# V by whole token tiles, one norm's transposes on VectorE through DRAM, and two chunks' head outputs split elsewhere, in a two-layer attention and Mish kernel

## The chip, the cores and the metric

The kernel runs on one core of one Trainium2 chip. The metric is the time of one execution on the device in microseconds (us), given as the median of several runs. PE is TensorE (the matrix engine), DVE is VectorE, ACT is ScalarE, POOL is GpSimd, and SP is SyncE, which here only issues DMAs.

## The reference

Everything is fp32. The sequence has 2048 tokens of width 512; there are 32 heads of width 16, and the hidden width of the dense part is 1792. The same weights serve both layers.

```python
def layernorm(x):  # no weights, eps 1e-5
    return (x - mean(x)) / sqrt(var(x) + eps)

def attention(x, wqkv, wo):
    q, k, v = (x @ wqkv) as 32 heads of 16
    p = softmax(q @ k.T * 16 ** -0.5)
    return heads(p @ v) @ wo

def dense(x, w1, b1, w2):
    h = x @ w1 + b1
    return (h * tanh(softplus(h))) @ w2      # Mish

x = A_x
for layer in range(2):
    x = x + attention(layernorm(x), A_wqkv, A_wo)
    x = x + dense(layernorm(x), B_w1, B_b1, B_w2)
```

## The kernel before, in words

**Tiles and precision.** Tokens are worked on in four chunks of 512 (NCH = 4), each of four tiles of 128. An fp32 product is made of three matmuls: each operand is split into a high part, rounded to the faster fp32r type, and a low part, the rest (`mm3`, L199 to L201: high by high, low by high or high by low). A split is a copy on ACT (or POOL) that makes the high part and a subtraction on DVE that makes the low part (`split_psum`, L193 and L194).

**Norm.** Two forms exist. `norm_parts` takes statistics on DVE (L228, L229), the inverse root on POOL (L210, L211), the scaled rows on DVE (L218), transposes them on PE (L248), and splits the result out of PSUM. `norm_units` does the same with DVE transposes (L298), stores on SP's queue to a DRAM buffer (L302), one load back (L311), and splits in SBUF (L314 on ACT, L315 on DVE). It is a generator whose steps are hung between other work. Its scaled and transposed tiles take places under the tag `raw` (three places), which every second projected tile `pt` of the next stage uses too.

**QKV.** `qkv` projects Q and K by pairs (m, c) in a written order: m is a group of 128 output features (0 to 3 are Q, 4 to 7 are K), c a token chunk. Each pair is one PSUM bank `qk` of twelve matmuls, split into `pt` (ACT, DVE) and stored to the DRAM buffer `scr` from ACT's queue. A dictionary `within` says ahead of which pair and step other functions run. In the second layer the first place where the last chunk (c = 3) is needed is the twelfth pair, (0, 3); its norm, called `late`, runs inside this order. V of chunks 0 to 2 follows (`va`); V of chunk 3 (`vp`, `v_parts` with `paired`) is drawn into the first steps of the attention. The function `behind` pins an instruction's place in the order; PE's instructions are chained in the written order in the second layer.

**Attention.** 8 groups of 4 heads, 4 query chunks, 16 key tiles of 128 make 512 steps (STEPS). Softmax subtracts a row maximum, which is worked out ahead of its use: a half step of maximum (`max_mm`, item M) makes two matmuls into one two-bank tile `pm` (tag `mx`, two buffers) and one DVE reduce (L404); every 32 of them end in `max_fold`. Score matmuls come in pairs (`sp`, L452, item P, tag `s2`) and singles (`ss`, L462, item S, tag `s1`), whose exp on ACT goes to `p` (L453, L463); `pv` matmuls (L478) sum p times V in one bank, which `drain` copies to `ot` (L499 to L503) and stores to `oscr`. Tiles `p` live in the shared pool of 8 KB places (`b8`), from which many other tiles come too, so that a `p` can take the place of any older tile. The items run in a fixed cycle of three steps. The pool of the score banks is opened with

```python
with tc.tile_pool(name="sa", bufs=1, space=PSUM, reuse_waits="tile") as self.pool:
```

At the attention's start, the first 2 PRE items M are not maxima but two `k` steps of V each (L520 to L522).

**Head outputs.** `HeadsOut` of a chunk loads the unnormalised sums (`num`) and the denominators (`den`) from `oscr`, inverts the denominators on DVE (`invert`, L664), sends them through DRAM (`rscr`) and spreads them over the features of each head (`spread`, `rec`), multiplies (L676), and splits into `oh` (POOL, L679) and `ol` (DVE, L680). Chunks 0 to 2 do this at hooks counted from the last step:

```python
for c, (t0, t1, t2, t3) in enumerate(((-42, -38, -36, -20), (-29, -21, -20, -13), (-13, -9, -8, None))):
```

They are the steps of load, inversion, spread and `parts` (product and split); chunk 2's `parts` come behind the loop. `project(c)` then multiplies by wo (`wo_parts`, 48 matmuls a chunk) and adds the residual (L718). The dense part follows, with hidden tiles `h` (L733) and output tiles `mo` (L759).

Of the kernel before, what the change touches and what calls it, by code (L numbers as in the profile page):

```python
# [18 lines left out]
P = 128  # L19
S, D, H, DH, F = 2048, 512, 32, 16, 1792  # L20
NCH = 4
# [57 lines left out]
def kernel(ctx: ExitStack, tc: tile.TileContext, x, wqkv, wo, w1, b1, w2, out):  # L79
# [244 lines left out]
    class Attention:  # L324
# [166 lines left out]
        def drain(self):  # L491
            b, self.full = self.full, None
            if b is None:
                return
            g, qb = divmod(b, NCH)
            ot = t512("f", f"ot{self.l}{b}")
            acc = self.accs.pop(b)
            if b == NG * NCH - 1:
                behind(nc.vector.tensor_copy(ot, acc))  # L499
            elif self.l and qb < NCH - 1:  # L500
                nc.scalar.activation(mixed(ot), grouped(acc), AF.Copy)  # L501
            else:
                nc.scalar.activation(ot, acc, AF.Copy)  # L503
            self.stored = nc.sync.dma_start(self.oscr[qb][g // 2, g % 2], ot)

        def run(self, hooks, pre):
# [3 lines left out]
            with tc.tile_pool(name="sa", bufs=1, space=PSUM, reuse_waits="tile") as self.pool:  # L510
                half, done = 2 * (AHEAD + PRE), -4
                for s in range(STEPS + 4):
                    if s % GSTEPS == GSTEPS - NKT and s // GSTEPS + 1 < NG:
                        self.prep_v(s // GSTEPS + 1)
                    for item in CYCLE[s % 3]:
# [3 lines left out]
                        elif item == "S":  # L519
                            self.single()  # L520
                        elif item == "M" and left:
                            left -= 1  # L522
                            next(pre)
                            next(pre)
                            if not left:
                                next(pre, None)
                                self.prep_v(0, [NCH - 1])
                        elif item == "M":
                            self.max_mm(half // 2, half % 2)
                            half += 1  # L530
                        else:
                            done += 1
                            self.pv(units(done))
# [113 lines left out]
    class HeadsOut:  # L647
# [14 lines left out]

        def invert(self):
            behind(nc.vector.reciprocal(self.den, self.den))  # L664
            for q in range(NCH):
                behind(nc.gpsimd.dma_start(self.rscr[:, ts(q, P)], self.den[ts(q, H)]))
# [6 lines left out]

        def parts(self):
            nm = f"{self.l}{self.c}"
            behind(nc.vector.tensor_tensor(self.num, self.num, self.rec, op=ALU.mult))  # L676
            oh = b8([P, KT, CW], F32R, "oh" + nm)
            ol = b8([P, KT, CW], F32R, "ol" + nm)
            nc.gpsimd.tensor_copy(oh, self.num)  # L679
            behind(nc.vector.tensor_tensor(ol, self.num, oh.bitcast(F32), op=ALU.subtract))  # L680
            self.out = oh, ol

        def pieces(self):
# [150 lines left out]
    for l in range(2):  # L834
# [10 lines left out]
        else:  # L845
            order = [(0, 0), (0, 1), (4, 0), (4, 1), (1, 0), (0, 2), (4, 2), (1, 1), (1, 2), (5, 0), (5, 1), (0, 3), (4, 3)]
            att = attention(1)
            att.chained = True
            late = norm_parts(x2s[NCH - 1], f"q1{NCH - 1}", tt, NCH - 1, "mx", True, pe=att.pe)
            for at in ((4, 0), (4, 0), (9, 0), (9, 2)):  # L850
                within.setdefault(at, []).append(lambda: next(late))
        order += [(m, c) for m in (1, 5, 2, 6, 3, 7) for c in range(NCH) if (m, c) not in order]
# [32 lines left out]
        outs = [HeadsOut(l, c, att.oscr) for c in range(NCH)]  # L885
        for c, (t0, t1, t2, t3) in enumerate(((-42, -38, -36, -20), (-29, -21, -20, -13), (-13, -9, -8, None))):
            o = outs[c]
            at(STEPS + t0, o.load)
            at(STEPS + t1, o.invert)
            at(STEPS + t2, o.spread)  # L890
# [8 lines left out]
        outs[3].load()  # L899
        outs[2].parts()  # L900
        load_res(1)
# [4 lines left out]
        load_res(3)  # L906
        for _ in project(0):
            pass
        first = norm_parts(x2s[0], f"m{l}0", tts, 0, "s", pin=behind, pe=att.pe, halves=True)
# [72 lines left out]
```

## Time and profile before

| | |
|---|---|
| Median of 3 runs | 3493.39 us (3493.02 to 3493.46) |
| Profiled execution | 3493.51 us |
| Its span | 3491.7 us |
| Granted TensorE clock, mean | 1.000 of full speed |
| PE busy | 3478.3 us, 100% of the span |
| DVE busy | 3001.3 us, 86% |
| ACT busy | 2572.9 us, 74% |
| POOL busy | 240.2 us, 7% |
| DMA | 274.99 MB, mean 79 GB/s |
| Largest groups | DVE max reduce L404 2384.2 us; ACT exp L453 1396.5 us; PE pv L478 1165.7 us; PE maximum L400 1099.0 us |

A group line of the profile reads: source line, engine, operation, output<-inputs with their shapes, how often, then its busy time and the mean of one, then the idle time of its engine ahead of it and what ended most of it. In a timeline row the first two numbers are the start and the duration in us; the bracket at the end is the idle time of the engine ahead of the row and what released it. Matmuls are pipelined, so the duration of one is longer than the distance to the next, and distances between starts are used for PE. Names without numbers stand for all tiles of that name.

### The profile page before, as it was taken

The numbers are of one execution on the slowest core, as the hardware profiler recorded it, in microseconds if no ns is written. First come the engines' busy times: TensorE is split into PE (matmuls) and PEld (weight loads), VectorE is DVE, ScalarE is ACT, GpSimd is POOL, SyncE is SP. The second block draws the span as 40 slices with busy tenths as digits, with TensorE's granted clock in tenths as the row PEclk, the third lists the DMA queues.
The fourth block names the chain that finished last, engine by engine and source line by source line (L and its number), as shares of the span: only waits on it lengthen the run. The fifth ranks groups of instructions, "written<-read, shape, count | busy, mean of one in ns | idle before, by whom it ended". The sixth has DMA issues, their size and how long they took to land.

```text
span 3491.7 us, 68687 instructions
## 1 busy us (share of the span) xinstructions
PE 3478.3 (100%) x28572; PEld 1921.3 (55%) x28572; DVE 3001.3 (86%) x3166; ACT 2572.9 (74%) x3513; POOL 240.2 (7%) x392
## 2 busy tenths in 40 slices
PE   9999999999999999999999999999999999999999
PEld 7644444444444444888876444444444444448887
DVE  6689999999999996667756999999999999956675
ACT  3288888888888889356622888888888888884565
POOL 3100010001001002100010000000000000021000
PEclk9999999999999999999999999999999999999999
DMA  7741323222131314722374203111120312156210
GB/s 248 234 91 44 64 60 75 50 53 72 51 63 56 65 36 91 231 69 73 109 224 151 45 21 58 34 35 34 32 48 21 54 27 45 21 113 213 76 37 25
DMA packets 185268, 274.99 MB, mean 79 GB/s; under 512 B 72117, under 2 KB 114037, under 8 KB 171133
## 3 DMA queue, kind: packets, MB, share of 16 engines
q1 hardware_dynamic: 158036, 193.95, 22.8%
q10 hardware_dynamic: 19176, 43.06, 3.6%
q0 software_dynamic: 7744, 33.60, 3.4%
q8 instruction: 224, 3.67, 0.5%
q14 instruction: 88, 0.71, 0.1%
HBM read 158.87 MB, written 110.62 MB: 77 GB/s over the span
## 4 chain that ended last, share of the span: by engine, by line
PE 96%; DMA 1%; DVE 1%; ACT 1%; issue 0%; POOL 0%; SPq 0%; DVEq 0%; ACTq 0%; POOLq 0%
PE pv L478 30%; PE pm L400 18%; PE ss L462 13%; PE sp L452 9%; PE h L733 8%; PE mo L759 8%; PE qk L199 2%; PE qk L200 1%; PE qk L201 1%; PE va L199 1%; PE wo L199 1%; PE wo L201 1%; PE wo L200 1%; PE va L201 1%; PE va L200 1%; DMA vscr<-v 0%
## 5 line engine op out<-in xcount | busy, mean ns | idle before, releaser
L404 DVE TENSOR_REDUCE mxv<-pm 128x2 f32<-128x1024 f32 x2048 | 2384.2, 1218 | 148.4 <-PE pm L400 96.0
L453 ACT ACTIVATE p<-sp 128x1024 f32<-128x1024 f32 x1366 | 1396.5, 1022 | 10.6 <-DMA vscr<-v 2.7
L478 PE MATMUL pv<-p,va 128*32 128x256 f32 (+2 forms) x16032 | 1165.7, 392 | 0.6 <-ACT ot L501 0.4
L400 PE MATMUL pm<-ks,qs 48*128 48x512 f32 x4096 | 1099.0, 446 | 1.6 <-DVE mxv L404 1.3
L463 ACT ACTIVATE p<-ss 128x512 f32<-128x512 f32 x1364 | 815.3, 598 | 338.6 <-PE ss L462 258.1
L452 PE MATMUL sp<-qs,ks 50*128 50x512 f32 x2732 | 738.1, 445 | 0.5 <-ACT p L453 0.5
L478 PEld LDWEIGHTS pv<-p,va 128*32 128x32 f32 x16032 | 368.3, 108 | 504.9 <-issue 424.4
L400 PEld LDWEIGHTS pm<-ks,qs 48*128 48x128 f32 x4096 | 451.8, 184 | 347.2 <-issue 234.1
L462 PE MATMUL ss<-qs,ks 50*128 50x512 f32 x1364 | 610.6, 448 | 1.5 <-ACT p L463 1.5
L462 PEld LDWEIGHTS ss<-qs,ks 50*128 50x128 f32 x1364 | 252.1, 185 | 329.4 <-ACT p L463 238.1
L452 PEld LDWEIGHTS sp<-qs,ks 50*128 50x128 f32 x2732 | 267.0, 183 | 184.4 <-ACT p L453 108.5
L421 POOL CAST hi<-nt 128x32 fp32r<-128x32 f32 x64 | 13.3, 208 | 2263.1 <-DVE nt L417 2263.1
L736 ACT ACTIVATE hb<-h,b1t 128x512 f32<-128x512 f32 x112 | 77.2, 689 | 101.6 <-PE h L733 100.7
L740 ACT ACTIVATE hr<-he 128x512 f32<-128x512 f32 x112 | 70.8, 632 | 104.6 <-DVE he L739 104.6
L193 ACT ACTIVATE pt<-qk 128x512 fp32r<-128x512 f32 x64 | 38.2, 597 | 143.4 <-PE qk L201 102.0
L743 DVE TENSOR_TENSOR hb<-hb,hr 128x512 f32<-128x512 f32 x112 | 77.4, 691 | 45.0 <-ACT hr L741 42.9
L737 DVE TENSOR_SCALAR he<-hb 128x512 f32<-128x512 f32 x112 | 47.5, 424 | 79.8 <-ACT hb L736 73.8
L747 DVE TENSOR_TENSOR al<-hb,ah 128x512 fp32r<-128x512 f32 x112 | 77.4, 691 | 28.8 <-ACT ah L746 23.1
L746 ACT ACTIVATE ah<-hb 128x512 fp32r<-128x512 f32 x112 | 70.2, 627 | 29.9 <-DVE hb L743 29.9
L739 DVE SCALAR_TENSOR_TENSOR he<-he 128x512 f32<-128x512 f32 x112 | 76.7, 685 | 17.2 <-ACT he L738 17.2
L194 DVE TENSOR_TENSOR pt<-qk,pt 128x512 fp32r<-128x512 f32 x64 | 43.8, 685 | 53.7 <-ACT pt L193 51.6
L741 ACT ACTIVATE hr<-hr,lnhalf 128x512 f32<-128x512 f32 x112 | 81.1, 724 | 3.6
(224 smaller groups left out, 3000.5 us busy)
## 6 DMA issues: line engine op xcount, KB each, us to landing
scr<-pt ACTq DMA_DIRECT2D x64, 512.0 KB
qs<-scr SPq DMA_DIRECT2D x174, 128.0 KB
ks<-scr SPq DMA_DIRECT2D x174, 128.0 KB
vscr<-v SPq DMA_DIRECT2D x32, 512.0 KB
va<-vscr SPq DMA_DIRECT2D x64, 256.0 KB
oscr<-ot SPq DMA_DIRECT2D x64, 256.0 KB
ww<-sw POOLq DMA_DIRECT2D x14, 1024.0 KB, 4.3
num<-oscr SPq DMA_DIRECT2D x64, 128.0 KB
```

Of the source, the lines that this page charges most:

```text
L199: pe(nc.tensor.matmul(acc, ah, bh, start=first and i == 0, stop=False))
L200: pe(nc.tensor.matmul(acc, ah, bl, start=False, stop=False))
L201: pe(nc.tensor.matmul(acc, al, bh, start=False, stop=last and i == n - 1))
L400: nc.tensor.matmul(pm[:, e], qs[u][rows, q0 : q0 + P], ks[u][rows, ts(n, 512)], start=True, stop=True)
L404: nc.vector.tensor_reduce(self.mxs[b][:, 2 * u : 2 * u + 2, qt, n], pm, axis=AX.X, op=ALU.max)
L452: self.pe(nc.tensor.matmul(sp[:, e], k, q, start=True, stop=True))
L453: nc.scalar.activation(self.pts[-1][:, 0:n], sp[:, 0:n], AF.Exp, scale=SCALE)
L462: self.pe(nc.tensor.matmul(sp, k, q, start=True, stop=True))
L463: nc.scalar.activation(self.pts[i // 3][:, 2], sp, AF.Exp, scale=SCALE)
L478: nc.tensor.matmul(self.accs[b][ts(h, VW), cols], self.va[b // NCH][:, kt, h, :], self.pts[j][:, e, cols], start=kt == 0 and q0 == 0, stop ...
L733: pe(nc.tensor.matmul(acc, w[:, part, k, ts(f % 2, P)], t[:, k, :], start=i == 0, stop=i == 3 * KT - 1))
L759: nc.tensor.matmul(obs[c][t // 2][:, t % 2], act[:, ts(t, P)], w[:, part, f % 2], start=f == part == 0 and act is ah, stop=f == FT - 1 and ...
```

## The change

1. V of the last chunk, both layers: in place of two `k` steps at each of the items M ahead of the maxima, all four `k` steps of one token tile (twelve matmuls) run at every second such item, and none at the others.
2. The second layer's last norm (`late`): `norm_units` takes the place of `norm_parts`; its steps run ahead of pairs 0 to 9 of the order.
3. Head outputs. Chunk 0's inversion is done in four quarters at four successive steps, and its spread moves from step −36 to −34. Chunk 1's product and split leave the loop (step −13) and come behind it, ahead of chunk 2's product; its cast moves from POOL to ACT. Chunk 2's split moves to the middle of the first projection.
4. In the second layer, `ot` is evicted through the `mixed` and `grouped` views for the fourth query chunk as well.

```diff
--- before.py
+++ after.py
@@ -495,12 +495,11 @@
             g, qb = divmod(b, NCH)
             ot = t512("f", f"ot{self.l}{b}")
             acc = self.accs.pop(b)
+            to, acc = (mixed(ot), grouped(acc)) if self.l else (ot, acc)
             if b == NG * NCH - 1:
-                behind(nc.vector.tensor_copy(ot, acc))
-            elif self.l and qb < NCH - 1:
-                nc.scalar.activation(mixed(ot), grouped(acc), AF.Copy)
+                behind(nc.vector.tensor_copy(to, acc))
             else:
-                nc.scalar.activation(ot, acc, AF.Copy)
+                nc.scalar.activation(to, acc, AF.Copy)
             self.stored = nc.sync.dma_start(self.oscr[qb][g // 2, g % 2], ot)
 
         def run(self, hooks, pre):
@@ -520,8 +519,8 @@
                             self.single()
                         elif item == "M" and left:
                             left -= 1
-                            next(pre)
-                            next(pre)
+                            for _ in range(KT * (left % 2)):
+                                next(pre)
                             if not left:
                                 next(pre, None)
                                 self.prep_v(0, [NCH - 1])
@@ -660,9 +659,10 @@
             for h in range(P // DH):
                 nc.sync.dma_start(self.num[ts(h, DH)], rows[:, h, 0:DH].rearrange("k d n -> d k n"))
 
-        def invert(self):
-            behind(nc.vector.reciprocal(self.den, self.den))
-            for q in range(NCH):
+        def invert(self, i=0, n=1):
+            part = ts(i, P // n)
+            behind(nc.vector.reciprocal(self.den[:, part], self.den[:, part]))
+            for q in range(NCH if i == n - 1 else 0):
                 behind(nc.gpsimd.dma_start(self.rscr[:, ts(q, P)], self.den[ts(q, H)]))
 
         def spread(self):
@@ -671,14 +671,23 @@
             for h in range(P // DH):
                 behind(nc.gpsimd.dma_start(self.rec[ts(h, DH)], rows[:, h][None].to_broadcast([DH, KT, CW])))
 
-        def parts(self):
+        def product(self):
+            return nc.vector.tensor_tensor(self.num, self.num, self.rec, op=ALU.mult)
+
+        def split(self, cast):
             nm = f"{self.l}{self.c}"
-            behind(nc.vector.tensor_tensor(self.num, self.num, self.rec, op=ALU.mult))
             oh = b8([P, KT, CW], F32R, "oh" + nm)
             ol = b8([P, KT, CW], F32R, "ol" + nm)
-            nc.gpsimd.tensor_copy(oh, self.num)
+            if cast is nc.scalar:
+                cast.activation(oh, self.num, AF.Copy)
+            else:
+                cast.tensor_copy(oh, self.num)
             behind(nc.vector.tensor_tensor(ol, self.num, oh.bitcast(F32), op=ALU.subtract))
             self.out = oh, ol
+
+        def parts(self):
+            behind(self.product())
+            self.split(nc.gpsimd)
 
         def pieces(self):
             nm = f"{self.l}{self.c}"
@@ -846,9 +855,9 @@
             order = [(0, 0), (0, 1), (4, 0), (4, 1), (1, 0), (0, 2), (4, 2), (1, 1), (1, 2), (5, 0), (5, 1), (0, 3), (4, 3)]
             att = attention(1)
             att.chained = True
-            late = norm_parts(x2s[NCH - 1], f"q1{NCH - 1}", tt, NCH - 1, "mx", True, pe=att.pe)
-            for at in ((4, 0), (4, 0), (9, 0), (9, 2)):
-                within.setdefault(at, []).append(lambda: next(late))
+            late = norm_units(x2s[NCH - 1], f"q1{NCH - 1}", tt, NCH - 1)
+            for n in (0, 0, 0, 0, 1, 2, 3, 4, 6, 8, 9):
+                within.setdefault((n, 0), []).append(lambda: next(late))
         order += [(m, c) for m in (1, 5, 2, 6, 3, 7) for c in range(NCH) if (m, c) not in order]
         qkv(l, att, wts, tt, order, within, due)
         if l == 0:
@@ -883,10 +892,12 @@
         for i in range(2):
             at(STEPS - 9 + 2 * i, lambda i=i: wot.append(ready(f"wo{i}", l)))
         outs = [HeadsOut(l, c, att.oscr) for c in range(NCH)]
-        for c, (t0, t1, t2, t3) in enumerate(((-42, -38, -36, -20), (-29, -21, -20, -13), (-13, -9, -8, None))):
+        for c, (t0, t1, t2, t3) in enumerate(((-42, -38, -34, -20), (-29, -21, -20, None), (-13, -9, -8, None))):
             o = outs[c]
             at(STEPS + t0, o.load)
-            at(STEPS + t1, o.invert)
+            n = NCH if c == 0 else 1
+            for i in range(n):
+                at(STEPS + t1 + i, lambda o=o, i=i, n=n: o.invert(i, n))
             at(STEPS + t2, o.spread)
             if t3 is not None:
                 at(STEPS + t3, o.parts)
@@ -897,15 +908,18 @@
         att.run(hooks, v_parts(l, NCH - 1, wts, tt, att, True))
         load_res(0)
         outs[3].load()
-        outs[2].parts()
+        behind(outs[1].product())
+        behind(outs[2].product())
+        outs[1].split(nc.scalar)
         load_res(1)
         load_w1(0)
         load_res(2)
         load_w2(0)
         load_w1(1)
         load_res(3)
-        for _ in project(0):
-            pass
+        for i, _ in enumerate(project(0)):
+            if i == NCH * KT // 2:
+                outs[2].split(nc.gpsimd)
         first = norm_parts(x2s[0], f"m{l}0", tts, 0, "s", pin=behind, pe=att.pe, halves=True)
         for i, _ in enumerate(project(1)):
             for n in range({0: 1, 8: 1, 11: 2, 14: 2}.get(i, 0)):
```

## The prediction

> **What bounds the kernel now.** I read the page first: busy shares, then the chain that ended last.
>
> ```profile
> span 3491.7 us, 68687 instructions
> PE 3478.3 (100%) x28572; PEld 1921.3 (55%) x28572; DVE 3001.3 (86%) x3166; ACT 2572.9 (74%) x3513; POOL 240.2 (7%) x392
> PE 96%; DMA 1%; DVE 1%; ACT 1%; issue 0%; POOL 0%; SPq 0%; DVEq 0%; ACTq 0%; POOLq 0%
> ```
>
> TensorE carries 96% of the chain and is idle for 13 us in all (3491.7 − 3478.3). So only two things can shorten the program: fewer or cheaper steps on PE, or the removal of a wait on PE. The change adds no matmul to PE and takes away only the 16 transposes of one norm. Everything else in it is worth what it does to PE's waits, and I looked at each place in the timeline by engine. The profiled execution took 3493.51 us, 1.81 around its span, and the median of the runs is 3493.39, so a difference worked out on the span is taken off the median as it stands. About 0.2% (7.0 us) is what a measurement of this kernel can tell from no change.
>
> **V by whole token tiles (both layers).** The timeline of PE in the second layer, where the last V chunk starts:
>
> ```profile
> 1896.56 0.50 PE L452 MATMUL sp<-qs,ks 50*128 50x512 f32 x2
> 1896.99 0.50 PE L199 MATMUL vp<-qkv4l,thq 128*128 128x512 f32 x1
> 1897.33 0.39 PE L200 MATMUL vp<-qkv4l,thq 128*128 128x512 f32 x1
> ...
> 1898.59 0.50 PE L462 MATMUL ss<-qs,ks 50*128 50x512 f32 x1
> ...
> 1902.99 0.49 PE L462 MATMUL ss<-qs,ks 50*128 50x512 f32 x1
> 1902.99 0.72 PE L452 MATMUL sp<-qs,ks 50*128 50x512 f32 x2
> 1903.65 0.50 PE L199 MATMUL vp<-qkv5l,thq 128*128 128x512 f32 x1
> ...
> 1915.67 0.50 PE L400 MATMUL pm<-ks,qs 48*128 48x512 f32 x2
> ```
>
> A block of six projection matmuls takes 1.60 us (1896.99 to 1898.59): the first step 0.34, against (1.60 − 0.34)/5 = 0.25 for the others. A block of twelve is then about 2.96. A lone sp between blocks costs 0.43 (1896.56 to 1896.99), ss and sp together only 0.66 (1902.99 to 1903.65). Four blocks of twelve for eight of six, with the score matmuls drawn together, would take some 2.2 us from the 19.11 us of this stage (1896.56 to 1915.67). But score matmuls side by side need their banks: ss and sp have one PSUM buffer each, so the next ss waits until ScalarE has read the last. ScalarE's rows:
>
> ```profile
> 1903.52 0.60 ACT L463 ACTIVATE p<-ss 128x512 f32<-128x512 f32 x1 [1.25 <-PE ss L462]
> 1904.02 1.02 ACT L453 ACTIVATE p<-sp 128x1024 f32<-128x1024 f32 x1
> ```
>
> An exp starts 0.53 after its ss and takes 0.60; the next sp's exp starts 0.50 later and takes 1.02. The new order is sp, 12, ss sp, 12, ss sp ss, 12, sp ss sp, 12, pv, ss sp, pv, pm. With zero at the first sp: first twelve 0.43 to 3.39; ss sp to 4.05; a wait of 0.15 for the V eviction; second twelve 4.2 to 7.16; ss 7.16, its exp 7.8 to 8.4, so the third ss starts at 8.45 where its place would be 7.82 (0.6 lost) and ends at 8.88; third twelve to 11.84; sp 11.84, its exp 12.49 to 13.51, so the sp after the next ss starts at 13.56 for 12.5 (1.05 lost), to 13.99; fourth twelve to 16.95; the rest (pv 0.78, ss sp 0.66, pv 0.78) ends at 19.17. Against 19.11 nothing is left of the saving. In the first layer one wait is in the trace already:
>
> ```profile
> 161.27 0.50 PE L452 MATMUL sp<-qs,ks 50*128 50x512 f32 x2
> ...
> 181.05 0.50 PE L400 MATMUL pm<-ks,qs 48*128 48x512 f32 x2
> 173.89 1.02 ACT L453 ACTIVATE p<-sp 128x1024 f32<-128x1024 f32 x1 [2.74 <-DMA vscr<-v]
> ```
>
> That exp waits for a store of V until 173.89, which is 12.6 after the first sp; in the new order its turn is at 12.5, so the wait falls together with the other one, and the stage is about 19.25 for 19.78. Sum of both layers: −0.5 us. Ends: −5.1 if no exp is waited for (2.2 and, with this wait gone, 2.9), +1.5 if the waits are longer by the 0.6 to 1.0 that I found for one of them.
>
> **Second layer's last norm.** PE loses two groups of eight transposes:
>
> ```profile
> 1776.75 1.03 PE L248 MATMUL tpq<-ident,xnq 128*128 128x128 f32 x8
> 1777.54 0.48 PE L199 MATMUL qk<-thq,qkv2l 128*128 128x512 f32 x1
> 1777.86 0.40 PE L200 MATMUL qk<-tlq,qkv2l 128*128 128x512 f32 x1
> ```
>
> Each costs 0.79 and a slow first matmul behind it (0.32 for the usual 0.23), together 1.8 us. In exchange the norm goes the way of the others: four transposes on VectorE, eight stores on SP's queue, a load, and four splits. Its price stands in an earlier norm of the trace:
>
> ```profile
> 1731.63 2.16 SPq L302 DMA_DIRECT2D ntq<-yq  x4
> 1735.81 0.38 SPq L311 DMA_DIRECT2D tlq<-ntq  x1
> 1739.98 1.14 ACT L314 ACTIVATE thq<-tlq 128x512 fp32r<-128x512 f32 x2
> 1763.25 0.17 DVE L229 BATCH_NORM_AGGREGATE mvq<-stq 128x2 f32<-128x6 f32 x1
> 1416.73 1.06 POOL L211 TENSOR_TENSOR rsm<-vem,mhalf 128x4 f32<-128x4 f32 x1
> ```
>
> Stats end at 1763.4, the root at about 1764.8 (1.06 and a short addition before it). The first half is turned by about 1767.2. The second half's tile takes a place that a pt leaves when its store to scr has landed, by my estimate 1770.4 to 1772, so it is turned by 1771.8 to 1773.3, and while VectorE waits there the pt splits queue behind it (0 to 0.75 us for PE, as the qk banks are three). Four issues take 2.2, the load is issued 2.0 after the last (1733.79 to 1735.81), and is used 4.2 later: 1780.2 to 1781.7, and to 1783 since the pt stores are on the same DMA engines. The group that needs this chunk, (0,3), now begins without the two transposes at 1776.75 + 2 × 2.72 = 1782.2. ScalarE has the eviction of the group just before ahead of the new splits: it cannot begin before 1782.4, and VectorE's split of the same tile stands before the first tl. So th at 1783.5, tl at 1784.4 (two evictions of a 512-wide bank at 0.60, as the exp above, and two VectorE splits that are not far from it): PE waits 2.2 us even if the load is early. Net +0.4, taken as +0.5. Ends: −1.8 (no wait) and +3.2 (a wait of 5, the load landing 3 us late).
>
> The Trainium skill (DMA: Bandwidth & Descriptors, Anatomy of one DMA) gives a DMA about 2.0 us fixed plus its bytes at 436 GB/s: 4.4 us for the 1 MB load, an estimate by that page. The trace's 4.17 agrees, so by that rule too the load lands in time and the wait is ScalarE's order.
>
> **First chunk's reciprocal in four.** It stands in the max loop:
>
> ```profile
> 1318.85 0.95 DVE L664 RECIPROCAL den<-den 128x128 f32<-128x128 f32 x1
> 1319.72 16.48 DVE L404 TENSOR_REDUCE mxv<-pm 128x2 f32<-128x1024 f32 x14
> 1319.78 0.50 PE L462 MATMUL ss<-qs,ks 50*128 50x512 f32 x1
> 1320.94 0.50 PE L400 MATMUL pm<-ks,qs 48*128 48x512 f32 x2 [0.67 <-DVE mxv L404]
> ```
>
> PE loses 1320.94 − 1319.78 − 0.22 (an ss in a run, 0.66/3) = 0.94, some 1.0 with what follows. A quarter would be 0.24 by length; but a VectorE instruction with almost no elements takes 0.17 (the aggregate above), so I give it 0.16 + 0.79/4 = 0.36, of which about 0.08 overlaps the next (0.95 held the reduce back by 0.87): 0.28. The 14 reduces behind it take 16.48, one each 1.18, and while work is waiting their starts are 1.13 apart; PE sends one each 1.20, so VectorE regains 0.14 for each pair. Followed reduce by reduce with two pm buffers, the four quarters cost PE 0.5, 0.2, 0.06 and 0.14, that is 0.87 for 1.0. With 0.20 for a quarter it is 0.6. I take −0.2 a layer, −0.4 in all; ends −2.0 (all hidden) and +0.4 (0.36 each without overlap).
>
> By the Trainium skill (VectorE: DVE Perf Modes, The TRN2 errata) each instruction that reads SBUF pays a fixed latency, with a measured term of about 150 cycles at 0.96 GHz (0.16 us): a rule against splitting. The 0.17 of the aggregate agrees; without the rule, by length alone, the sum would be −0.8.
>
> **Second chunk behind the attention.** In both layers an exp waits for that chunk's product, since its p tile takes the place of the chunk's reciprocals:
>
> ```profile
> 1376.73 1.02 ACT L453 ACTIVATE p<-sp 128x1024 f32<-128x1024 f32 x1 [1.00 <-DVE num L676]
> 3111.93 1.02 ACT L453 ACTIVATE p<-sp 128x1024 f32<-128x1024 f32 x1 [1.01 <-DVE num L676]
> 1378.30 0.50 PE L462 MATMUL ss<-qs,ks 50*128 50x512 f32 x1 [0.75 <-ACT p L463]
> ```
>
> Here ScalarE paces the loop, so its 1.00 is lost but for what PE had in hand. PE shows 0.75 idle. I take 0.8, between the two and nearer to PE's own row. In the new program that tile's place comes from the first chunk's product, which is long done. Gain 2 × 0.8 = 1.6. What becomes due later is the work behind the attention:
>
> ```profile
> 1400.82 0.69 DVE L499 COPY ot<-pv 128x512 f32<-128x512 f32 x1 [18.88 <-PE pv L478]
> 1402.24 2.29 DVE L676 TENSOR_TENSOR num<-num,rec 128x2048 f32<-128x2048 f32 x1 [0.73 <-DMA rec<-rscr]
> 1406.67 2.29 DVE L680 TENSOR_TENSOR ol<-num,oh 128x2048 fp32r<-128x2048 f32 x1 [2.14 <-POOL oh L679]
> 1404.74 1.90 POOL L679 CAST oh<-num 128x2048 fp32r<-128x2048 f32 x1 [8.55 <-issue]
> 1411.70 0.39 PE L199 MATMUL wo<-wo0l,oh 128*128 128x512 f32 x1
> ```
>
> New order on VectorE: copy to 1401.5, product of chunk 1 to 1403.8, of chunk 2 to 1406.0 (its reciprocals land at 1402.2), low part of chunk 1 (ScalarE's cast 1403.9 to 1405.8, taken as POOL's 1.90) to 1408.3, a residual add, then chunk 2's low part to about 1411.8. PE needs chunk 1 at 1411.7, 3.4 us later than it is ready, and chunk 2 another 10.9 later. So this work stays hidden by the projection of chunk 0; if that cover failed, each us behind 1411.7 would cost one. Chunk 0's later reciprocal DMAs and the exchange of SP's loads have tens of us to spare, and the evictions of ot through another view cost the same. Gain −1.6; end 0 if another slot takes over the wait.
>
> **Sum.** −0.5 + 0.5 − 0.4 − 1.6 = −2.0: 3493.4 − 2.0 = 3491.4 us.
>
> **Rivals.** Faster: ScalarE keeps ahead and no exp, split or reciprocal is waited for. Then −5.1 − 1.8 − 2.0 − 1.6 = −10.5, 3482.9 us. The single banks speak against it, PE's present slack in the stage for it; it counts as faster from 3486.4 down, that is if the V stage gives nearly all. Chance 0.15.
>
> Slower: the norm's round trip through DRAM. VectorE runs in order: while the second half's transposes wait for a place, the pt splits behind them stop, PE stops for a bank, and so the next pt store, which frees places, comes later too. Two such rounds of 2.72 and a load among the stores put the wait at (0,3) near 13 us: −2.5 − 1.8 + 13 = +8.7, 3502.1 us. From a wait of 11.3 it is slower by 0.2%; from 4.3 it eats all gain. Against it: the earlier norm's trip took 8.3 us from stores to use, and 19 us lie between stats and need. Chance 0.10. By the Trainium skill (TensorE: Matmul & The Clock Gate, What's actually happening) PE idle for a window of about 3.4 us falls to half its clock; no run here shows it, as no wait on PE is that long, and by that page such a wait would cost some 1.7 us more, an estimate.
>
> The third is that nothing net is left: the V stages end at their old length plus 1.5, the exp waits elsewhere, 3493.4 to 3495. It lies within 0.2%, with the forecast: 0.75 together, of which the forecast's own 3488.5 to 3493.4 has some 0.5.
>
> The range for 8 in 10 reaches into both outer cases: 3484.5 to 3499.
>
> **What would show it.** First sp to first pm: 19.2 in both layers, with PE waiting for exps of about 0.6 and 1.05 in place of shorter ones. At (0,3): a wait of about 2.2 on DVE tl. The cycle with the reciprocal at 0.6 to 0.9 over the others. No DVE num ahead of an exp; first wo of chunk 1 without a wait. Wrong would be a V stage under 18 us, a wait at (0,3) under 1 or over 5, or a new wait in the projections.

## The result

The changed kernel takes 3499.43 us (median; 3496.50 to 3501.20) against 3493.15 (3492.41 to 3494.58): ratio 1.0018, interval 1.0011 to 1.0025. It is 6.3 us slower. The forecast was 3491.4 with a range up to 3499.0, so the time lies just above the range, and on the other side of the kernel before. Within the 0.2% that the prediction called "no change" it lies at the edge, but the interval leaves no doubt of the sign.

The head of the page of the changed kernel:

```profile
span 3497.3 us, 68661 instructions
...
PE 3477.8 (99%) x28556; PEld 1923.1 (55%) x28556; DVE 3004.4 (86%) x3178; ACT 2577.7 (74%) x3517; POOL 237.8 (7%) x384
...
PE 96%; DMA 2%; DVE 1%; ACT 1%; issue 0%; POOL 0%; SPq 0%; DVEq 0%; ACTq 0%; POOLq 0%
```

PE is as busy as before (3477.8), but the span is 5.6 us longer: PE waits 19.5 us in place of 13.4, and DMA's share of the chain rose from 1% to 2%. Where it went is seen when the starts of the same PE instructions are set against each other. Each row is the shift that a stage adds (changed minus before, in the two profiled executions, 3499.04 and 3493.51):

| Stage | forecast | measured |
|---|---|---|
| First layer, up to the first sp | 0 | +0.36 |
| First layer, last V chunk | −0.5 | −0.44 (19.78 to 19.34) |
| First layer, loop up to the reciprocal | 0 | +0.27 |
| First layer, reciprocal | −0.2 | −0.45 |
| First layer, second chunk in the loop | −0.8 | −0.86 |
| First layer, projections | 0 | −0.33 |
| Second layer, QK up to the end of (0,3) | +0.5 | **+6.85** |
| Second layer, from there to the first sp | 0 | +0.77 |
| Second layer, last V chunk | +0.06 | +0.05 (19.11 to 19.16) |
| Second layer, loop up to the reciprocal | 0 | −0.24 |
| Second layer, reciprocal | −0.2 | −0.36 |
| Second layer, second chunk in the loop | −0.8 | −0.90 |
| Second layer, projections | 0 | +0.84 |

The program up to the first sp is the same in all kernels here but one, and its length still differs by −0.14 to +1.21 from profile to profile, so rows of a few tenths are read with that in mind.

One row decides. The timelines of SP's queue, ScalarE and PE in that stretch, changed kernel (the last row is the first matmul of the next pair):

```profile
1765.39 8.34 SPq L302 DMA_DIRECT2D ntq<-yq  x8
1777.72 0.38 SPq L311 DMA_DIRECT2D tlq<-ntq  x1
...
1781.66 0.60 ACT L193 ACTIVATE pt<-qk 128x512 fp32r<-128x512 f32 x1 [2.66 <-PE qk L201]
...
1786.06 2.19 ACT L314 ACTIVATE thq<-tlq 128x512 fp32r<-128x512 f32 x4 [3.80 <-DMA tlq<-ntq]
...
1786.74 0.80 PE L199 MATMUL qk<-thq,qkv0l 128*128 128x512 f32 x1 [5.12 <-ACT thq L314]
1787.46 0.80 PE L200 MATMUL qk<-tlq,qkv0l 128*128 128x512 f32 x1
1788.06 0.63 PE L201 MATMUL qk<-thq,qkv0l 128*128 128x512 f32 x1
1788.48 0.63 PE L199 MATMUL qk<-thq,qkv0l 128*128 128x512 f32 x1
...
1792.11 0.40 PE L199 MATMUL qk<-thq,qkv2l 128*128 128x512 f32 x1
```

The first matmul of the same pair, and of the next, in the kernel before:

```profile
1783.98 0.39 PE L199 MATMUL qk<-thq,qkv0l 128*128 128x512 f32 x1
...
1786.70 0.39 PE L199 MATMUL qk<-thq,qkv2l 128*128 128x512 f32 x1
```

The load is issued 4.0 us after the issue of the last store has ended (1773.73 to 1777.72) and used 8.3 us after its issue. PE is idle for 5.12 us at pair (0,3), and its next matmuls come 0.4 to 0.7 us apart in place of 0.23. The same stretch by windows (the columns are the window, its length, PE, PEld, DVE, ACT and POOL busy with counts, the granted clock, the DMA engines' share, GB/s), first the changed kernel, then the one before:

```profile
1767.00:1772.00 5.00, 5.00 (x24) 4.14 (x23) 2.00 (x3) 0.81 (x2) 0.00 (x0) 1.00 0.98 272
...
1777.00:1782.00 5.00, 4.62 (x21) 3.50 (x19) 0.69 (x1) 0.94 (x2) 0.00 (x0) 1.00 0.85 272
1782.00:1787.00 5.00, 0.26 (x1) 0.26 (x1) 0.97 (x2) 1.20 (x3) 0.00 (x0) 0.80 0.94 348
1787.00:1792.00 5.00, 5.00 (x12) 3.61 (x13) 2.82 (x5) 1.73 (x4) 0.00 (x0) 0.51 0.31 117
```

```profile
1767.00:1772.00 5.00, 5.00 (x24) 4.13 (x23) 1.08 (x2) 1.09 (x2) 0.00 (x0) 1.00 0.65 239
...
1777.00:1782.00 5.00, 5.00 (x32) 4.33 (x31) 2.78 (x3) 3.15 (x4) 0.00 (x0) 1.00 0.44 168
```

Two things are to be seen: the DMA engines went from 0.4 to 0.65 busy to 0.85 to 0.98, and the granted clock fell to 0.51 behind the wait. The pair's twelve matmuls took 5.37 us (1786.74 to 1792.11) in place of 2.72, which is 2.65 us beside the 5.12 of the wait. Not all of the 2.65 is the clock: at a clock of 1.00 the same pair takes 3.34 us when it has to follow the splits one by one (the run with idle matmuls, below), so some 2.0 us are the clock and 0.6 the splits.

### The profile page after: what moved, and what is told of

The parts are those of the page before. It is cut to its first block, busy times and chain, and to the rows that moved or that the text cites. A ratio compares the mean times of both kernels' runs of the same rounds, so it can differ in the third digit from the quotient of the medians.

```text
span 3497.3 us, 68661 instructions
## 1 busy us (share of the span) xinstructions
PE 3477.8 (99%) x28556; PEld 1923.1 (55%) x28556; DVE 3004.4 (86%) x3178; ACT 2577.7 (74%) x3517; POOL 237.8 (7%) x384
## 4 chain that ended last, share of the span: by engine, by line
PE 96%; DMA 2%; DVE 1%; ACT 1%; issue 0%; POOL 0%; SPq 0%; DVEq 0%; ACTq 0%; POOLq 0%
PE pv L478 30%; PE pm L400 18%; PE ss L462 13%; PE sp L452 9%; PE h L742 8%; PE mo L768 8%; PE qk L199 1%; PE qk L200 1%; PE qk L201 1%; PE wo L199 1%; PE wo L201 1%; PE wo L200 1%; PE va L199 1%; PE va L201 1%; PE va L200 1%; DMA vscr<-v 0%
```

## The experiments

Medians stand beside the kernel before on the same chip (3493.0 to 3493.6).

**The late norm alone, and all but it.** The edit moves one part:

```diff
-            late = norm_parts(x2s[NCH - 1], f"q1{NCH - 1}", tt, NCH - 1, "mx", True, pe=att.pe)
-            for at in ((4, 0), (4, 0), (9, 0), (9, 2)):
-                within.setdefault(at, []).append(lambda: next(late))
+            late = norm_units(x2s[NCH - 1], f"q1{NCH - 1}", tt, NCH - 1)
+            for n in (0, 0, 0, 0, 1, 2, 3, 4, 6, 8, 9):
+                within.setdefault((n, 0), []).append(lambda: next(late))
```

(`norm_units` leaves the tokens of its chunk in another order than `norm_parts`, and the fourth part of the change, the view of `ot`, goes with it. In these two kernels the view of the fourth query chunk is not the one that fits, so tokens of that chunk are exchanged; the work is the same.)

> The kernel before with one part of the change: the second layer's last norm by norm_units. Theory A (the whole loss sits in this part: in the changed kernel PE waited 5.12 us at pair (0,3) and then ran 12 matmuls at a granted clock of 0.51, 2.65 us too long, against 1.6 us of transposes saved; PE's time there moved from -1.43 to +5.42): about +7 us, 3500, with a wait of 4 to 6 us at (0,3), a granted clock near 0.5 behind it and a wait of about 0.7 ahead of the first sp of the attention. Rival B (the wait comes out of the parts together, for example since the attention's and the V stage's edits shift the DMA traffic): under +3 us, a wait under 3 us and no fall of the clock.

Measured: 3501.94 for 3493.51, ratio 1.0025 (1.0015 to 1.0034), +8.4 us. The profile repeats the changed kernel's:

```profile
1787.84 0.79 PE L199 MATMUL qk<-thq,qkv0l 128*128 128x512 f32 x1 [5.39 <-ACT thq L314]
...
1903.98 0.57 PE L452 MATMUL sp<-qs,ks 50*128 50x512 f32 x2 [0.69 <-ACT v L638]
```

> The changed kernel with the second layer's last norm put back to norm_parts; all other edits stay. Theory A: the gains of the other parts are left, first layer -1.4, second layer V 0, reciprocal -0.4, second chunk -0.9 and +0.8 from the residual load that comes late for the first norm behind it: about -2, 3491.2, no wait over 1.2 us on PE in the second layer's projections, clock 1.000. Rival B (the other parts lose too): 3493 or more.

Measured: 3491.76 for 3493.51, ratio 0.9996 (0.9987 to 1.0005). Theory A holds in both: this part carries the loss, and the 0.69 ahead of the first sp belongs to it too (it is in every kernel with this norm, in none without; what makes ScalarE late there was not looked into). Two details of the second forecast did not come: the residual load took back 0.1 us and not 0.8, and the clock fell once, in the first layer's V stage. Both are taken up below.

**Is the clock's part real?** Twelve idle matmuls ahead of (0,3):

```diff
+            def fill():
+                acc = ps.tile([P, 2, 512], F32, tag="mx", name="fill")
+                th, _ = tt[0]
+                for i in range(12):
+                    att.pe(nc.tensor.matmul(acc[:, 0], wts[0][:, 0, i % KT, 0:P], th[:, i % KT], start=True, stop=True))
+
+            within.setdefault((11, 0), []).append(fill)
```

> The changed kernel with twelve matmuls of 512 columns whose result nobody reads, ahead of pair (0,3) in the second layer. They take 2.7 us of the 5.1 us in which PE is idle there. Theory A (the fall of the clock follows from the length of PE's idle time): 2.4 us idle, granted clock 1.00 behind it, 2.65 us less than the changed kernel, about 3496.8. Rival B (the clock falls for another reason, for example any wait over 1 to 2 us): the clock still falls, 3499.4. Rival C (the extra matmuls delay the data too): 3502.

Measured: 3497.45, 2.0 less than the changed kernel's 3499.43 (each against its own before: +3.9 and +6.3). PE's row at the place in the timeline, and the window behind it:

```profile
1786.26 0.49 PE L199 MATMUL qk<-thq,qkv0l 128*128 128x512 f32 x1 [1.23 <-ACT thq L314]
```

```profile
1787.00:1792.00 5.00, 5.00 (x22) 4.16 (x23) 3.03 (x5) 1.85 (x4) 0.00 (x0) 1.00 0.33 124
```

The clock stays at 1.00, and (0,3) takes 3.34 us in place of 5.37 (its later steps still follow the splits one by one). PE is idle for 1.23 and not for the 2.4 that theory A had, since in this profile the load is also used 1.2 us sooner after the start of the stage (1785.58 − 1743.44 = 42.1, for 43.4); that is no part of what the edit does. Theory A at this place: work that nobody needs, put into the gap, is worth 2 us. The median moved by as much, but five of the ten executions, 3497.4 to 3499.0, have a mean clock of 0.999 on record, which points to a fall somewhere in about half of them; the profile (3495.83) is one of the others.

**Is the chunk only late?** Two more pairs ahead of the need:

```diff
-            order = [..., (5, 0), (5, 1), (0, 3), (4, 3)]
+            order = [..., (5, 0), (5, 1), (5, 2), (2, 0), (0, 3), (4, 3)]
```

> The changed kernel with pairs (5,2) and (2,0) moved ahead of (0,3) and (4,3): the normed chunk is needed 2 x 2.72 = 5.4 us later. Theory A (the chunk is only late by the 5.1 us): the wait at (0,3) is under 0.5 us, the clock stays at 1.00, 3499.4 - 5.1 - 2.65 = 3491.7. Rival B (the stores of two more projected tiles ahead of the load on the same DMA engines push its landing back by as much): a wait of 2 to 5 us, 3494 to 3499.

Measured: 3497.30. The figures are in rival B's range, the reason is neither theory's: the load is used as long after the start of the stage as before (43.6 us for 43.4), and ScalarE's order came in between. The profile is the longest of ten executions (3495.49 to 3499.63).

```profile
1787.51 2.19 ACT L314 ACTIVATE thq<-tlq 128x512 fp32r<-128x512 f32 x4 [3.97 <-DMA tlq<-ntq]
1789.60 1.55 ACT L193 ACTIVATE pt<-qk 128x512 fp32r<-128x512 f32 x3
...
1791.33 0.79 PE L199 MATMUL qk<-thq,qkv0l 128*128 128x512 f32 x1 [2.99 <-DVE pt L194]
```

The splits stand ahead of the evictions of the two new pairs, ScalarE waits in order for the load, and PE waits 2.99 us for a bank; the clock falls again (0.78 in the window from 1792). So the splits were moved too, from pairs 8 and 9 to 11 and 12:

```diff
-            for n in (0, 0, 0, 0, 1, 2, 3, 4, 6, 8, 9):
+            for n in (0, 0, 0, 0, 1, 2, 3, 4, 6, 11, 12):
```

> The changed kernel with pairs (5,2) and (2,0) ahead of (0,3), as before, and besides with the norm's four splits moved from pairs 8 and 9 to pairs 11 and 12, so that ScalarE no longer waits for the norm's load ahead of evictions that PE needs. Theory A (with the need put off, what was left was ScalarE's order: PE waited 2.99 us for a pt split behind it, and the clock fell): a wait of 0.5 to 1 us at (0,3), granted clock 1.00, 3497.3 - 2.2 - about 2 = 3493. Rival B (the load itself is still late): wait of 2 us or more, 3495 to 3497.

Measured: 3494.81 for 3493.13. At the place itself theory A holds (wait 0.83, clock 1.00), but the total misses its 3493: from the start of the second layer's QK to the first sp the program loses 3.2 us all the same (a shift of −1.6 against the kernel before, then +1.7). Of these 2.4 come behind the first maximum, where the trace has waits of 0.76 and 0.69; the rest was not followed up. Putting off the use of the chunk is no cure.

**Why is it late: places or DMA?** First the norm's tiles in places of their own (the call passes `own=True`; without it the tiles are as before):

```diff
+            if own:
+                both = b8([P, 2, 2 * D], F32, f"xy{nm}{h}")
+                xn = both[:, 0].rearrange("p (t d) -> p t d", t=2)
+                y = both[:, 1].rearrange("p (b j r) -> p b j r", j=2, r=TR)
...
```

> The changed kernel with the late norm's scaled and turned tiles in the shared pool of 8 KB places, not under the tag raw: VectorE's second pair of transposes no longer waits for a pt store (1.77 us idle at 1770.45 in the changed kernel). Theory A (the chain is late first of all for want of a place, and DMA traffic adds to it): the second half is turned 2 to 3 us earlier, the load lands about 2 us earlier, PE's wait at (0,3) falls from 5.1 to about 3, below where the clock fell, so 3499.4 - 2 - 2.65 = about 3494.8. Rival B (the DMA engines set the end whatever the order: stores of 256 bytes, pt stores and the load need 19 of 22 us): wait still 4.5 to 5.5, clock falls, 3499.

```profile
1770.94 7.98 SPq L307 DMA_DIRECT2D ntq<-xyq  x8
1782.79 0.38 SPq L316 DMA_DIRECT2D tlq<-ntq  x1
...
1788.89 0.80 PE L199 MATMUL qk<-thq,qkv0l 128*128 128x512 f32 x1 [4.60 <-ACT thq L319]
```

Measured: 3501.57 for 3493.64. A miss for theory A; the wait and the clock are B's (4.60, 0.52), and the total is 2.6 above B's 3499 (in the profile 1.7 went to a fall of the clock in the first layer's V stage). The reason isn't quite B's, though: with the places free the scheduler mixed the two halves, so that the first store left 26.5 us after the start of the stage (1770.94 − 1744.40) in place of 22.7, and the load at 1782.79; it was then used 5.4 us after its issue, as most pt stores were through (0.8 us of all 16 engines in that time, for 4.0 in the changed kernel). Places alone settle nothing.

Then less store traffic: the low parts of nine pt tiles are not stored. (The rest of the edit declares the second layer's buffers ahead of the first layer and writes the constants there.)

```diff
+            a1 = 1 if l and 2 <= n <= 10 else 2
             nc.scalar.dma_start(
-                scr[m][:, :, ts(c, CW)].bitcast(F32).rearrange("a p n -> p a n"), pt.bitcast(F32)
+                scr[m][0:a1, :, ts(c, CW)].bitcast(F32).rearrange("a p n -> p a n"), pt[:, 0:a1].bitcast(F32)
             )
```

> The changed kernel with the low parts of nine projected tiles of the second layer (pairs 2 to 10 of the order) not stored; constants written far earlier stand in their place, so the output is not the reference's. The pt stores' work on the DMA engines falls from 10.3 us to about 6 in the stretch of the late norm. Theory A (the chain is late by contention): the norm's stores take less than their 9.7 us, the load is used 5 to 6 us after its issue in place of 8.3, and the wait at (0,3) falls from 5.1 to 1 to 2.5 us without a fall of the clock: about 3493.5. Rival B (stores of 256 bytes and a load are as slow by themselves): wait 4 to 5, 3498.

Measured: 3503.06, a miss in the total: 8.8 us went at the very start of the first layer (its first pm comes at 189.84 for 181.05), where this kernel differs by the earlier declaration of the second layer's buffers; that was not followed up. The place in question can be read all the same, in the timelines of SP's queue, ScalarE and PE:

```profile
1785.63 0.38 SPq L311 DMA_DIRECT2D tlq<-ntq  x1
...
1792.12 2.19 ACT L314 ACTIVATE thq<-tlq 128x512 fp32r<-128x512 f32 x4 [6.13 <-DMA tlq<-ntq]
...
1792.81 0.50 PE L199 MATMUL qk<-thq,qkv0l 128*128 128x512 f32 x1 [2.01 <-ACT thq L314]
```

The load is used 6.5 us after its issue in place of 8.3, the wait is 2.0, and the clock stays up: theory A at this place. Shorter stores also leave their places sooner, so this run doesn't part places from traffic. The last test takes the stores out of the way without leaving any out. They are kept back, in the shared pool, until the norm's load has landed:

```diff
-            if n % 2:
+            if n % 2 or (l and 2 <= n <= 10):
...
+            if l and 2 <= n <= 10:
+                held.append(store)
+            else:
+                store()
+            while held and n >= 10:
+                held.pop(0)(pin=behind)
```

> The changed kernel with the stores of nine projected tiles of the second layer (pairs 2 to 10) held back until the norm's load has landed; the tiles have places of their own in the shared pool meanwhile, so the norm's transposes do not wait for a place either. Theory A (the wait of 5.1 us at (0,3) comes from sharing the DMA engines and the places with the pt stores; the norm's way through DRAM alone takes what it takes in the dense part, 4.2 us from the last stores to the load and 4.2 from the load to its use): the load is used by about 1780, before PE needs it, the wait at (0,3) is under 1 us, no fall of the clock; up to (0,3) the second layer then gains the 1.6 us of the transposes, 3499.4 - 5.1 - 2.65 = 3491.7, if the stores that now come in one run do not delay the first maxima. Rival B (the norm's own stores of 256 bytes and its load are slow whatever runs beside them): wait of 3 us or more, 3496 to 3499.

The same timelines of this kernel:

```profile
1766.84 4.43 SPq L302 DMA_DIRECT2D ntq<-yq  x8
1773.63 0.38 SPq L311 DMA_DIRECT2D tlq<-ntq  x1
...
1778.63 2.19 ACT L314 ACTIVATE thq<-tlq 128x512 fp32r<-128x512 f32 x4 [2.50 <-DMA tlq<-ntq]
1780.78 0.39 PE L199 MATMUL qk<-thq,qkv0l 128*128 128x512 f32 x1
...
1781.50 9.12 ACTq L597 DMA_DIRECT2D scr<-pt  x8
...
1792.04 0.50 PE L199 MATMUL qk<-thq,qkv2l 128*128 128x512 f32 x1 [2.94 <-DVE pt L194]
```

Measured: 3496.88 for 3492.97, a miss for theory A's total (3491.7) though not for its wait. The eight stores of the norm now take 4.43 us at the queue in place of 8.34, the load is issued 2.4 later and used after 5.0, and PE does not wait at (0,3) at all (1780.78, the fourth row): it is 3.2 us ahead of the kernel before there, 1.4 of them from the first layer and 1.8 within the stage, where the transposes are gone. That settles the cause: the norm was late because it shared places and DMA engines with the pt stores. Counted from the start of the stage the load is used 7.4 us sooner; 2.5 of these are gained up to the last of the norm's stores, where VectorE no longer waits for a place, and 5.0 on the two DMA legs behind it. The gain is lost behind it: eight stores of 512 KB in a row keep ScalarE's own queue for 9.12 us, evictions wait, PE waits 2.94, and the clock falls to 0.66 in the next window.

**The other parts alone.** V by whole token tiles:

```diff
-                            next(pre)
-                            next(pre)
+                            for _ in range(KT * (left % 2)):
+                                next(pre)
```

> The kernel before with V by whole token tiles alone, in both layers. By the prediction's step: second layer 19.17 us from the first sp to the first pm (19.11 before), first layer about 19.3 (19.78 before), total -0.5, 3493.0; the waits for exps of 0.5 and 1.0 in both. Rival (the blocks' saving of 2.2 us a layer comes through where ScalarE has less else to do): 3489.

Measured: 3494.23 for 3493.64, ratio 1.0001 (0.9992 to 1.0010). In the second layer the stage takes 19.14, as forecast; in the first one 21.02, for the 19.34 of the changed kernel. PE's row behind the wait, and two windows, cut where the granted clock changes:

```profile
175.62 0.50 PE L452 MATMUL sp<-qs,ks 50*128 50x512 f32 x2 [1.32 <-ACT p L453]
```

```profile
172.65:176.07 3.42, 2.10 (x11) 0.98 (x9) 0.00 (x0) 2.11 (x3) 0.00 (x0) 1.00 0.99 299
176.07:179.48 3.41, 3.41 (x10) 2.73 (x9) 0.00 (x0) 1.02 (x1) 0.00 (x0) 0.50 0.24 52
```

The wait for the exp is the same (1.2 to 1.4 us in all nine profiles that have this order), but here, and in two more of the nine, the clock fell behind it; the stage then takes 21.0 to 21.1, otherwise 19.3 to 19.6.

What makes the difference can be seen in the traces. In all profiles here the granted clock changes only at steps of 3.41 us: it is down for one step here, and for two (1785.03 to 1791.86) in the changed kernel's second layer. The wait falls into these steps differently from execution to execution. In the three profiles with a fall, PE is busy for 2.00 to 2.10 us of the step ahead of it (0.59 to 0.61); in the other six, no step around the wait has less than 2.13 (0.62). Busy time alone is not the whole rule, since steps of dense matmuls at the programs' end, busy for 0.44 to 0.54, brought no fall, while the score matmuls of the V stage use 50 of 128 rows. No run moved the wait against the steps, so this is read off the profiles and not tested.

With five idle matmuls in that gap:

```diff
+            if self.l == 0 and i == 12:
+                spare = ps.tile([P, 2, 512], F32, tag="mx", name="fill")
+                ks, qs = self.qk[0]
+                for _ in range(5):
+                    self.pe(nc.tensor.matmul(spare[:, 0], qs[0][0:KROWS, 0:P], ks[0][0:KROWS, 0:512], start=True, stop=True))
```

> The kernel before with V by whole token tiles alone, and in the first layer five score-sized matmuls whose result nobody reads, at the place where PE waited 1.3 us for an exp (1.1 us of them). In the profile of V alone the granted clock fell behind that wait (seven projection matmuls 0.43 apart in place of 0.23) and the first layer's stage took 21.0 us; in the changed kernel's profile it did not fall and took 19.34. Theory A (the wait brings the fall, in part of the executions): no fall, stage 19.3, 3494.2 - 1.1 = 3493.1, and runs closer together. Rival B (the fall comes from the load on PE in general): stage 21 again, 3494.2 or more.

```profile
173.00:177.00 4.00, 3.72 (x18) 2.32 (x17) 0.00 (x0) 3.13 (x4) 0.00 (x0) 1.00 0.74 224
177.00:181.00 4.00, 4.00 (x36) 2.07 (x34) 0.00 (x0) 1.44 (x4) 0.00 (x0) 1.00 0.61 166
```

Measured: 3492.95 for 3493.13, the stage 19.34 at a clock of 1.00. Theory A fits: against the kernel before, +0.6 became −0.2 (medians; both intervals hold 1). That no execution falls any more is not shown by one profile, and the runs are hardly closer together (3492.28 to 3494.32, for 3492.82 to 3495.10).

**The head outputs alone** (the third part of the diff on the kernel before):

> The kernel before with the head outputs' edits alone (reciprocal in quarters, second chunk behind the attention, third chunk's split in the first projection). From the changed kernel's trace: -0.4 a layer from the reciprocal, -0.9 a layer from the second chunk: -2.6, 3490.9. Rival (in the second layer the residual's load sets the first norm behind the attention, so that its 0.9 is given back): -1.8, 3491.7.

Measured: 3492.14 for 3493.64, ratio 0.9996 (0.9986 to 1.0005). In the profile, the longest of ten executions, the reciprocals gave 0.38 and 0.37, the second chunk 0.82 and 0.87, and the second layer's projections took 1.26 back: the rival. The rows of the give-back, DVE's and PE's in the timeline:

```profile
3153.80 1.23 DVE L728 TENSOR_TENSOR x<-wo,x 128x1024 f32<-128x1024 f32 x1 [1.69 <-DMA x<-xs]
...
3155.53 0.66 PE L264 MATMUL tpm<-ident,xnm 128*128 128x128 f32 x4 [1.14 <-DVE xnm L218]
```

The first norm stands behind the residual's add, and that behind a load which waits its turn at SP's queue. It is a matter of tenths: with the same order of loads the projections took 0.7 to 1.3 us longer than before in seven profiles, but only 0.1 in the changed kernel with the old norm and 0.0 in the one with twelve idle matmuls; the late norm alone, without the heads' edits, took 0.6 longer too. How the load falls among other traffic thus counts beside these edits. So the loads were exchanged:

```diff
         load_res(0)
+        load_res(1)
         outs[3].load()
         behind(outs[1].product())
         behind(outs[2].product())
         outs[1].split(nc.scalar)
-        load_res(1)
```

> The kernel before with the head outputs' edits alone, and the residual load of the second chunk issued ahead of the fourth chunk's head loads. In the run with the head outputs' edits alone the second layer gained 0.87 us up to the end of the attention and gave back 1.26 in the projections, where the first norm waits for that load. Theory A (the order of the loads does it): nothing is given back, 3492.1 - 0.8 = 3491.3. Rival B (the loads are bound by the DMA engines as a whole, or the fourth chunk then comes late): 3492 or more.

SP's queue and PE in the timeline of this kernel:

```profile
3134.70 1.00 SPq L871 DMA_DIRECT2D x<-xs  x2
...
3152.60 0.60 PE L264 MATMUL tpm<-ident,xnm 128*128 128x128 f32 x4
```

Measured: 3490.96 (3489.91 to 3491.22) for 3493.13 (3491.99 to 3494.16), ratio 0.9993 (0.9984 to 1.0002). The wait is gone and nothing is given back in this profile, and no execution is longer than 3491.22, where the old order reached 3493.97. Against its own before, the median gained 0.7 us over the old order (−2.2 for −1.5), less than the two intervals can tell apart. This is the version that beats both kernels, by 2.2 us and by some 8; its times and those of before do not overlap, though the interval just reaches 1.

## Why the prediction was wrong, point by point

**V by whole token tiles: right.** The waits were put at 0.6 and 1.05 and the end at 19.17; the changed kernel waits 0.52 and 0.99 in the second layer and ends at 19.16. The rows of the trace and the single banks gave this to a few hundredths. In the first layer 19.34 was measured for 19.25. What the step lacked is the clock: behind the 1.3 us wait it can be halved for 3.4 us, and the part alone then comes out at about +0.6 and not −0.5.

**The last norm: the step that failed.** Up to the second half's transposes the working held (done at 1771.76, which is 1773.2 in the times of the kernel before, as the stage starts 1.43 earlier; forecast 1771.8 to 1773.3). Then "the load is issued 2.0 after the last (1733.79 to 1735.81), and is used 4.2 later: 1780.2 to 1781.7, and to 1783 since the pt stores are on the same DMA engines" was mis-sized. The legs took 4.0 and 8.3, the use came at 1786.1 (1787.5 in those times). I had read both legs off a norm in the dense part, where next to nothing but the load itself was on the engines meanwhile, and put the sharing at some 1.3 us, though the DMA rows of this stretch could be added up: packets of the pt stores, the 4096 packets of 256 bytes and the load together need 10.3, 5.4 and 3.5 us of all 16 engines, 19 of the 22 us from 1765 to 1787. With the pt stores held back the legs are 2.4 and 5.0. Sharing is not the whole of it, as the second leg was 6.5 with half the stores gone and only 0.7 us of them beside the load; that spread stays open. So the wait was 5.1 in place of 2.2, as long as the upper end that the step had given (5, net +3.2), and it ended with the load (3.80 <-DMA at ScalarE) and not with ScalarE's order, as the step had it. Where the load was early, with the stores held back, the 2.2 were not there either: the splits ran ahead of the eviction that the step had put before them (from 1778.63), and PE did not wait.

Above that bound stands the price of the clock. It was in the prediction as a sentence of its own and in no sum. The Trainium skill (TensorE: Matmul & The Clock Gate, What's actually happening) says that PE falls to half its clock after an idle window of about 3.4 us. The trace agrees for the long wait: 5.12 us idle, then a granted clock of 0.51, at a cost of some 2.0 us, where the estimate by that page was 1.7. The idle matmuls, which left a gap of 1.23, kept the clock in the profiled execution. The waits of 1.3 us in the V stage, with the clock down behind them in three of nine profiles, show that a gap well under 3.4 us can do it. The step forecast +0.5; 5.12 − 2.2 and the pair's 2.65 bring it to about +6, and 0.7 ahead of the first sp, which I had not seen at all, to 6.8 of the table's 6.85 + 0.77.

The Trainium skill (DMA: Bandwidth & Descriptors, Anatomy of one DMA) gave an estimate of 4.4 us for the load, by a fit that the page states for DMAs issued by GpSimd, while this load is issued by SP. The measured 8.3 differs, and the measurement decides: the sum of a fixed time and the load's own bytes has no term for the 4.0 us of stores that were on the engines beside it.

**The rival.** The slower rival named the right place (the round trip through DRAM), and its "from 4.3 it eats all gain" was met by the wait of 5.1. Its mechanism was right in one half alone, the load among the stores. The other half, two rounds of 2.72 in which VectorE holds up the pt splits and PE, was not there: VectorE waited 1.77 us for a place once, and PE 0.41 for it at most. So its wait of 13 was too high.

**Reciprocal in quarters: right in kind, the size off.** A quarter takes 0.34 (forecast 0.36) and holds the next reduce back by 0.27 (0.28):

```profile
1319.04 0.35 DVE L664 RECIPROCAL den<-den 128x32 f32<-128x32 f32 x1
1319.31 2.29 DVE L404 TENSOR_REDUCE mxv<-pm 128x2 f32<-128x1024 f32 x2
1321.51 0.34 DVE L664 RECIPROCAL den<-den 128x32 f32<-128x32 f32 x1
1321.77 2.29 DVE L404 TENSOR_REDUCE mxv<-pm 128x2 f32<-128x1024 f32 x2
```

By the starts of PE's maxima the first quarter costs PE 0.54 in the first layer (forecast 0.5) and the other three 0.06 in all, for the 0.2, 0.06 and 0.14 that I gave them: the gain is 0.36 to 0.45 a layer for 0.2. Four quarters take 1.38 for the one of 0.95, about 0.14 more for each added instruction; the fixed latency of the Trainium skill (VectorE: DVE Perf Modes, The TRN2 errata), 0.16 by the page, is borne out by this.

**Second chunk behind the attention: right where it was looked for** (0.86 and 0.90 for 0.8). "So this work stays hidden" held for the head outputs, but the residual's load, which comes through the same queue, was no term ("the exchange of SP's loads" was to have "tens of us to spare"): it gave back 0.84 in the changed kernel's second layer and 1.26 with this part alone, though not in every profile.

## What to carry to other kernels

A transfer's price from a quiet stage is not its price in a busy one: add up the engine time of every queue's packets over the stretch between start and need, and where that nears the stretch's length, take a wait into the sum. Where PE paces the kernel, a wait can have two prices, the wait itself and the half clock behind it, and a cheap way to find out which is to fill the gap with idle matmuls. When a gain is had on the critical path, look for the load that was timed to the old end; here one line of the issue order seems to have brought back what it took, some 0.7 us.

## What was not expected of the hardware

The granted clock fell behind a wait of only 1.3 us, in three of nine profiles with waits of 1.2 to 1.4 at the same place, and cost some 1.7 us (stages of 21.0 to 21.1 for 19.3 to 19.6). Whether it fell went with how the wait lay in the clock's steps of 3.41 us. Eight DMA issues in a row on ScalarE's queue held that engine for 9.1 us, at a DMA share of 1.05. A 1 MB load took 8.3 us from issue to use beside 4.0 us of other stores on the engines, 5.0 with those held back.
